# The opening of a recurrence-and-feed-forward kernel, rewritten as an order by hand

## The chip, the cores and the metric

One core of one Trainium2 chip runs the whole kernel. The metric is device time in microseconds, the median of three runs. Kernel inputs are float32 or float64 (the two weights of the first feed-forward layer are float64 and arrive as pairs of 32-bit words). The engines are TensorE (matrix products, PE in the rows), VectorE (DVE), ScalarE (ACT), GpSimd (POOL) and the queue that starts most transfers (SP). Each executes its own instructions in program order.

## The reference

```python
for t in range(S):                      # attention part: 4 batches, 8 heads, 768 steps, 48 wide
    cur = einsum('bhd,bhe->bhde', u[None] * kt, vt)
    y[:, :, t] = einsum('bhd,bhde->bhe', rt, state + cur)
    state = wt[:, :, :, None] * state + einsum('bhd,bhe->bhde', kt, vt)
x = y.transpose(0, 2, 1, 3).reshape(3072, 384)
h = x @ w_in                            # 384 x 2048
x = (h * sigmoid(1.702 * h)) @ w_out    # 2048 x 384
# then: a gate picks one of 8 experts per token, 384 tokens each,
# in order of the logits, and each expert is relu(x @ w1[e]) @ w2[e]
```

## The kernel before, in words

The tokens are cut into 24 **units** of 128 (a chunk of time of one batch) and 8 **blocks** of three units. A unit turns r, k, v, w into 128 rows of x:

- VectorE: two running products of w (the scans, L837 into `Q` and L841 into `Fw`), r*k for the diagonal (L853), k scaled by `Q` (L857), r scaled by `Fw` (L860);
- TensorE: the diagonal (L872), copied by ScalarE to `dg` (L873) and laid on a diagonal by GpSimd (L893); the 128x128 products of k and r (L909); the transposes of k (L928);
- VectorE merges the products into `At` above the diagonal (L916);
- TensorE multiplies `At` with v (L1003, L1009); ScalarE rounds the result to the high part `xh` (L1022) and VectorE subtracts for the low part `xl` (L1024). The state for the next chunk of the batch comes from L945 and L957.

The dense layer then runs block by block, in 16 steps f. A step is a first product `g1` (L1087, nine matmuls: high by high, high by low, low by high), a gelu with a new split into `gh` and `gl` (L1133, L1136, L1139), and a second product `g2` (L1115). Block 0 runs eight steps, then all 16 of block 1, then the rest of block 0.

The weights come in 16 float64 chunks, W0 to W15, alternately of w_in and w_out, 768 KB each. Step f takes the chunk pair f // 2. `split64` turns a chunk into a high and a low float32 part: ScalarE reads the high words (L727), VectorE makes two passes over them (L731, L734) and two over the low words (L740, L741), ScalarE rounds the high part (L745). For W0 to W7 the remainder is formed by TensorE in two halves, three products each (L753 to L755), and moved back by ScalarE (L758); from W8 on VectorE does it (L768, L775).

What stands where in the program is set at build time. `Issue` is a planner: each unit and each chunk is a generator that yields what its last piece costs, and the planner resumes it when its estimate of the engines says so. While it has nothing for TensorE it inserts small products on an identity matrix, `spin` (L691), which keep the engine active and compute nothing that is used. The transfers of the start are in the order of a string:

```python
    ORDER = "0wkr 1wkr W0 2wkr 0v 1v W1 2v 3wkrv 6m"
```

(digits are units, letters their inputs.) The raw chunks land in two buffers `raw64`, so W2 is loaded when W0 is split (L636, through `load_w(m + 2)`). At most eight transfers of the queues are under way: each waits for the landing of the eighth before it.

Of the kernel before, what the change touches and what calls it, by code (L numbers as in the profile page):

```python
# [21 lines left out]
C = 128  # L22
# [478 lines left out]
def kernel(ctx, tc, r, k, v, w, rk, u, us, w_in, w_out, w_gate, w1, w2, out):  # L501
# [44 lines left out]
    LASTF = 3  # L546

# [91 lines left out]

# [17 lines left out]
    ORDER = "0wkr 1wkr W0 2wkr 0v 1v W1 2v 3wkrv 6m"  # L657
    for x in ORDER.split():
        if x[0] == "W":
# [14 lines left out]
    lead = s1p.tile([R2, HP * PW + 1], U8, name="lead")  # L674
    V.memset(lead, 0)
    V.memset(lead[:, ::PW], 1)
    lead2 = s1p.tile([R2, HP * PW], F32, name="lead2")
    V.memset(lead2, 0.0)
# [26 lines left out]

    def split64():
# [3 lines left out]
        def chain(m):  # L710
            while m not in raws:
                yield 0.2
            yield from arrived("raw", m)
            while begun[0] < m:
# [4 lines left out]
            raw = raws.pop(m)  # L719
            low = raw.bitcast(U32).rearrange("p (n two) -> p n two", two=2)[:, :, 0]  # L720
            high = raw.bitcast(I32).rearrange("p (n two) -> p n two", two=2)[:, :, 1]
# [5 lines left out]
            A.activation(a, high.bitcast(F32), AF.Abs, scale=2.0 ** -112)  # L727
            begun[0] = m + 1
            yield (("A", 0.9),)
            yield from sc.room("V", 0.3)  # L730
# [10 lines left out]
            V.scalar_tensor_tensor(Wlo[key] if m < NPE else b, low, 2.0 ** -52, b, op0=OP.mult, op1=OP.mult)  # L741
            if m < NPE:
# [5 lines left out]
                load_w(m + 2)  # L748
# [17 lines left out]
            load_w(m + 2)  # L766
# [13 lines left out]
        for m in range(len(wq)):  # L780
            sc.add(chain(m), SRANK if m < 8 else 2.7)
# [34 lines left out]

    def unit(un):
# [857 lines left out]
```

## Time and profile before

| | |
|---|---|
| median of 3 runs | 852.58 us (852.16 to 854.24) |
| the profiled execution, own time | 854.69 us |
| its span, first to last instruction | 852.7 us |
| TensorE busy | 828.5 us, 97% |
| VectorE busy | 594.6 us, 70% |
| first product of the dense layer (L1087) starts | 39.34 us |
| step f = 2 of block 0 starts | 52.70 us |
| block 1 starts | 107.21 us |

TensorE is nearly always busy by this table, but its busy time holds the `spin` products and whatever runs at half clock. The share of an engine says little on the opening, which is why the times of three landmarks stand beside it: from L1087's first row on, TensorE has the dense layers to do, and before that it waits for x and for weights.

### The profile page before, as it was taken

How to read it: one execution, taken by the hardware profiler on the slowest of the kernel's cores; microseconds unless marked ns; L12 is line 12 of the kernel's file. 1: busy time of each engine (PE TensorE's matmuls, PEld its weight loads, DVE VectorE, ACT ScalarE, POOL GpSimd, SP SyncE). 2: the span in 40 equal slices, each digit the busy share in tenths (PEclk: the TensorE clock that was granted, in tenths of full speed). 3: DMA queues.
4: the chain of work that ended last, by engine and by line, in shares of the span. 5: the costliest groups of instructions: out<-in, count | busy, mean ns of one | idle time of the engine just before them, and what ended most of it. 6: DMA issues, size and time to landing. Idle time of an engine off the chain costs nothing.

```text
span 852.7 us, 17604 instructions
## 1 busy us (share of the span) xinstructions
PE 828.5 (97%) x6789; PEld 776.2 (91%) x6789; DVE 594.6 (70%) x1584; ACT 354.6 (42%) x688; POOL 140.5 (16%) x197
## 2 busy tenths in 40 slices
PE   7999999999999999999999999999999999999996
PEld 6788899999999999999999999997988998999995
DVE  8577578868777775775776856377888887875310
ACT  2254564333233334333333233403566555665521
POOL 3100000010100100100000000002333344445211
PEclk9899999999999999999999999999999999999998
DMA  9623443252321331321322100006989799989400
GB/s 268 178 86 112 162 124 101 64 186 79 112 80 45 104 89 53 96 80 56 103 81 70 46 4 28 1 20 173 225 233 278 214 213 286 264 205 348 98 28 28
DMA packets 46211, 107.04 MB, mean 126 GB/s; under 512 B 7368, under 2 KB 13360, under 8 KB 46128
## 3 DMA queue, kind: packets, MB, share of 16 engines
q1 hardware_dynamic: 30960, 69.26, 25.6%
q0 software_dynamic: 10416, 29.50, 15.8%
q10 hardware_dynamic: 4752, 7.17, 2.3%
q8 instruction: 53, 0.87, 0.4%
q14 instruction: 30, 0.25, 0.1%
HBM read 74.78 MB, written 10.03 MB: 99 GB/s over the span
## 4 chain that ended last, share of the span: by engine, by line
PE 83%; issue 6%; DMA 5%; DVE 3%; ACT 1%; POOL 1%; SPq 0%; POOLq 0%; ACTq 0%; DVEq 0%
PE g L1087 31%; PE acc L1115 31%; PE s L909 3%; PE s L1003 3%; PE s L424 2%; DMA cvb<-x2d,idx 2%; PE s L753 1%; PE s L998 1%; DMA raw<-in_w_out 1%; PE s L1240 1%; PE g L1583 1%; PE acc L691 1%; PE s L945 1%; PE s L1251 1%; PE s L928 1%
## 5 line engine op out<-in xcount | busy, mean ns | idle before, releaser
L1115 PE MATMUL acc<-wk,gh 128*128 128x384 f32 x1080 | 283.3, 341 | 0.1
L1115 PEld LDWEIGHTS acc<-wk,gh 128*128 128x128 f32 x1080 | 192.6, 188 | 3.9 <-issue 3.0
L1115 PE MATMUL acc<-wk,gl 128*128 128x384 f32 x540 | 181.9, 337 | 0.0
L1087 PE MATMUL g<-xha,wk 128*128 128x384 f32 x576 | 167.5, 340 | 0.0
L1087 PE MATMUL g<-xhb,wk 128*128 128x384 f32 x576 | 166.7, 340 | 0.2 <-DVE hold L1139 0.2
L1133 ACT ACTIVATE g<-g 128x384 f32<-128x384 f32 x128 | 60.8, 475 | 212.1 <-PE g L1087 207.7
L1139 DVE TENSOR_TENSOR gl<-g,gh 128x384 fp32r<-128x384 f32 x116 | 64.1, 553 | 64.2 <-ACT gh L1136 63.3
L1087 PEld LDWEIGHTS g<-xhb,wk 128*128 128x128 f32 x576 | 105.8, 189 | 0.8 <-DVE hold L1139 0.5
L1087 PEld LDWEIGHTS g<-xha,wk 128*128 128x128 f32 x576 | 105.6, 188 | 0.5
L1115 PEld LDWEIGHTS acc<-wk,gl 128*128 128x128 f32 x540 | 101.4, 188 | 0.0
L893 POOL TENSOR_SCALAR_AFFINE_SELECT At<-dg 128x512 f32<-128x512 f32 x42 | 31.4, 770 | 414.1 <-DVE dg L886 381.9
L1087 PE MATMUL g<-xlb,wk 128*128 128x384 f32 x288 | 97.4, 338 | 0.0
L1087 PE MATMUL g<-xla,wk 128*128 128x384 f32 x288 | 97.1, 337 | 0.0
L1164 DVE SCALAR_TENSOR_TENSOR cvb<-cva,raw 128x384 f32<-128x384 f32 x144 | 79.3, 551 | 9.6 <-ACT cva L1203 7.3
L1146 ACT ACTIVATE gh<-g 128x384 fp32r<-128x384 f32 x64 | 31.4, 490 | 92.8 <-PE g L1087 86.4
L1149 DVE SCALAR_TENSOR_TENSOR gl<-g,gh 128x384 fp32r<-128x384 f32 x64 | 35.3, 552 | 41.8 <-ACT gh L1146 41.1
L1136 ACT ACTIVATE gh<-g 128x384 fp32r<-128x384 f32 x116 | 57.0, 491 | 7.1 <-ACT cva L1203 2.4
L1466 POOL DMA_DIRECT2D wk<-hold x51 | 46.3, 1014 | 67.4 <-ACT wk L1458 51.9
L1441 ACT ACTIVATE wk<-hold 128x768 fp32r<-128x768 f32 x64 | 52.9, 840 | 7.3 <-DMA hold<-in_w 7.3
L1087 PEld LDWEIGHTS g<-xlb,wk 128*128 128x128 f32 x288 | 54.3, 188 | 0.8 <-issue 0.6
L1087 PEld LDWEIGHTS g<-xla,wk 128*128 128x128 f32 x288 | 54.2, 188 | 0.0
L279 DVE TENSOR_TENSOR cvc<-c,raw 128x768 bf16<-128x768 bf16 x98 | 49.5, 553 | 1.3
(236 smaller groups left out, 1177.1 us busy)
## 6 DMA issues: line engine op xcount, KB each, us to landing
hold<-in_w SPq DMA_DIRECT2D x64, 384.0 KB
wk<-hold POOLq DMA_DIRECT2D x51, 384.0 KB
nat_m<-in_rk SPq DMA_DIRECT2D x18, 384.0 KB
raw<-in_w_in SPq DMA_DIRECT2D x8, 768.0 KB
raw<-in_w_out SPq DMA_DIRECT2D x8, 768.0 KB
nat_v<-in_v SPq DMA_DIRECT2D x22, 256.0 KB
nat_w<-in_w SPq DMA_DIRECT2D x22, 226.2 KB
nat_k<-in_k SPq DMA_DIRECT2D x22, 224.0 KB
```

Source lines behind the costliest of these rows:

```text
L279: self.nc.vector.tensor_tensor(g[:, x:x + step, :n].rearrange("p j (a b) -> p j a b", b=2), self.pairs(c[:, j:j + step], n), self.numbers( ...
L893: P.affine_select(At[s], dg[:, s::2][:, :, None].to_broadcast([128, HP, C]), pattern=[[0, HP], [1, C]], compare_op=OP.is_equal, fill=0.0, ...
L1087: T.matmul(p, self.l1(kt, f, a), (self.xh, self.xl)[b_][:, kt], start=(kt == 0 and n == 0), stop=(kt == KT - 1 and n == 2))
L1115: T.matmul(self.acc[tt], gs[a][:, tt * C:(tt + 1) * C], self.r2(f, b_), start=(f in self.cuts and n == 0), stop=(end and n == 2))
L1133: A.activation(p, p, AF.Gelu_apprx_sigmoid)
L1136: A.activation(gh, p, AF.Copy)
L1139: V.tensor_tensor(gl, p, gh.bitcast(F32), op=OP.subtract)
L1146: A.activation(gh, p, AF.Relu)
L1149: V.scalar_tensor_tensor(gl, p, 0.0, gh.bitcast(F32), op0=OP.max, op1=OP.subtract)
L1164: V.scalar_tensor_tensor(scr[0][:, 0], x2, 1.0, wgB[e // 4][:, (e % 4) * Dm:(e % 4 + 1) * Dm], op0=OP.mult, op1=OP.mult, accum_out=router. ...
L1441: A.activation(Whi[key], raw, AF.Copy)
L1466: P.dma_start(out=Wlo[key].bitcast(F32), in_=raw, accum_op=OP.add)
```

## The change

The first three units leave the planner. A new generator `first_unit` holds what a unit of block 0 does, in pieces, and a string says which piece of which unit (0, 1, 2) or of which chunk (W0, W1) is put next, how many `spin` products go between (s60), and to what the planner's clock is set (@9):

```diff
+    FIRST = ("@9 0 0 s60 0 s4 0 0 1 1 s22 1 0 1 s5 0 2 1 0 0 @16 W0 2 1 2 2 s2 1 1 @20 W0 1 W1 2 2 "
+             "@24 W0 W0 s16 2 2 2 @26 W1 W0 W0 W0 @28")
...
+    APART = 2, 3
...
-        raw = cv.tile([128, KT * CW], I64, name="raw64", bufs=2)
-        nc.sync.dma_start(raw, (w_in if name == "in" else w_out)[i])
-        raws[m] = raw
+        src = (w_in if name == "in" else w_out)[i]
+        if m in APART:
+            n = KT * CW // 2
+            rings = [R["wk"].new() for _ in range(2)]
+            raw = [wpool.tile([128, KT * CW], F32, name="wk") for _ in range(2)]
+            for h in range(2):
+                nc.sync.dma_start(raw[h].bitcast(I32), src[:, h * n:(h + 1) * n].bitcast(I32))
+            raws[m] = raw, rings
+        else:
+            raw = cv.tile([128, KT * CW], I64, name="raw64", bufs=2)
+            nc.sync.dma_start(raw, src)
+            raws[m] = [raw], []
...
+    def next_raw(m):
+        if m not in APART:
+            load_w(m + (4 if m < APART[0] else 2))
...
-    nc.scalar.dma_start(uB, dram(u, 0, [[0, 128], [1, Dm]]))
-    nc.scalar.dma_start(usel, us)
-    ORDER = "0wkr 1wkr W0 2wkr 0v 1v W1 2v 3wkrv 6m"
+    ORDER = "0wkr us 1wkr 0v 2wkr W0 1v 2v W1 W2 W3 3wkrv uB 6m"
...
+    lead = s1p.tile([R2, HP * PW + 1], U8, name="lead")
+    V.memset(lead, 0)
+    V.memset(lead[:, ::PW], 1)
+    lead2 = s1p.tile([R2, HP * PW], F32, name="lead2")
+    V.memset(lead2, 0.0)
     ident = consts.tile([128, 128], F32, name="ident")
...
             begun[0] = m + 1
             yield (("A", 0.9),)
+            while split[0] < min(m, INTURN):
+                yield 0.1
             yield from sc.room("V", 0.3)
             V.tensor_scalar(ai, ai, 3, None, op0=OP.logical_shift_left)
-            yield (("V", 0.56),)
-            yield from sc.room("V", 0.3)
-            V.scalar_tensor_tensor(ai, high, -2147483648, ai, op0=OP.bitwise_and, op1=OP.bitwise_or)
-            yield (("V", 0.99),)
+            for x, c_ in zip(high, cut):
+                V.scalar_tensor_tensor(ai[:, c_], x, -2147483648, ai[:, c_], op0=OP.bitwise_and,
+                                       op1=OP.bitwise_or)
+            yield (("V", 1.55),)
...
-                load_w(m + 2)
+                next_raw(m)
...
     def get_part():
-        while (1, NU - 1) not in stored:
+        while (1, NU - 1) not in stored or split[0] < len(wq):
             yield 0.2
...
     def paced(un):
-        while slot[0] < start[un] or NU - 1 not in half:
+        while slot[0] < start[un] or split[0] < INTURN:
             yield 0.2
...
+    for x in FIRST.split():
+        if x[0] == "s":
+            spin(int(x[1:]))
+        elif x[0] == "@":
+            sc.t = float(x[1:])
+        else:
+            piece(x)
...
-    sc.until(lambda: xdone.get(0) == NU)
...
+        fine[0] = s < begin[2]
```

`first_unit` has the instructions of the old `unit` for a direct unit, with three differences: the products of k and r go into the accumulators of the dense layer (`acc1`, `acc2`) and the output products into a buffer of the first product (`g1`), so that they take none of the three shared buffers `s`; the transposes of k stand right behind the products of k and r; and no `spin` stands inside a group of products. `unit` itself loses its branches for the first three units, and all later units now have the form that only units from 3 on had before (each group of products in one piece). W2 and W3 arrive in two halves each, in buffers of their own, at the start; W4 and W5 then follow W0 and W1. The four passes of VectorE over one chunk of W0 to W3 stand together, since the next chunk waits for its turn. New line numbers: load L618, raw load L652 (halves L648), `spin` L714, first read of a chunk L758, VectorE's passes L764, L766, L773, L775, rounding L783, three products L791 to L793, back L796, scans L874 and L878, r*k L886, diagonal L890, k and r scaled L901 and L902, products L909, transposes L915, merge L922, output products L929 and L933, xh L941, state L946, xl L953, `g1` L1190, `g2` L1218.

On VectorE, from the merge of unit 1 to the first product's last inputs, before:

```order
L916 COPY_PREDICATED wk<-later,s_365 128x512
L916 COPY_PREDICATED wk<-later,s_366 128x512
L853 TENSOR_TENSOR At_401<-wk 112x512
L734 SCALAR_TENSOR_TENSOR cvc<-raw_115,cvc 128x768
L1024 TENSOR_TENSOR xlb<-s_393,xhb 128x3x128
L857 TENSOR_TENSOR wk<-wk,Q 112x512
L860 TENSOR_TENSOR wk<-wk,Fw 112x512
L740 TENSOR_SCALAR cvb<-cvc 128x768
L741 SCALAR_TENSOR_TENSOR wk<-raw_115,cvb 128x768
L916 COPY_PREDICATED At_401<-later,s_462 128x512
L916 COPY_PREDICATED At_402<-later,s_463 128x512
```

and after (cvc, cvb and raw are chunk W0's; At_401 and At_378 are unit 2's):

```order
L922 COPY_PREDICATED wk<-later,acc_316 128x512
L922 COPY_PREDICATED wk<-later,acc_317 128x512
L886 TENSOR_TENSOR At_378<-wk 112x512
L901 TENSOR_TENSOR wk<-wk,Q 112x512
L902 TENSOR_TENSOR wk<-wk,Fw 112x512
L764 TENSOR_SCALAR cvc<-cvc 128x768
L766 SCALAR_TENSOR_TENSOR cvc<-raw_118,cvc 128x768
L953 TENSOR_TENSOR xlb<-g_397,xhb 128x3x128
L922 COPY_PREDICATED At_378<-later,acc_393 128x512
L922 COPY_PREDICATED At_379<-later,acc_394 128x512
L773 TENSOR_SCALAR cvb<-cvc 128x768
L775 SCALAR_TENSOR_TENSOR wk<-raw_118,cvb 128x768
```

Unit 2's scaling of k and r no longer stands behind the wait for unit 1's xh (L1024), and W0's last two passes have moved behind unit 2's merge.

On TensorE, from unit 2's products of k and r (L909) to the dense layer's first product, after (the rows left out are repeats, and 16 `spin` products between L793 and L929):

```order
L909 MATMUL acc_394<-wk 128x128
L915 MATMUL s_439<-ident,wk 128x112 x4
L791 MATMUL s_454<-cvc,ident 128x384
L792 MATMUL s_454<-wk,identr_148 128x384
L793 MATMUL s_454<-wk,identr_147 128x384
...
L929 MATMUL g_474<-At_378,wk 64x128 x2
L933 MATMUL g_474<-At_379,wk 64x128 x2
...
L946 MATMUL s_488<-wk,kn 48x48
L791 MATMUL s_502<-cvc,ident 128x384
L792 MATMUL s_502<-wk,identr_148 128x384
L793 MATMUL s_502<-wk,identr_147 128x384
L1190 MATMUL g_507<-xhb,wk 128x384
```

Before, the two halves of W0's remainder stood between the thirds of unit 2's output products, and its state products (L945) came after the first product had begun. Now one half stands ahead of all output products of unit 2, the other and the state products behind them, all ahead of the first product.

On the queue SP, from the 4th entry on, before (`wk` are unit 2's inputs, `raw` are W0 and W1, the number behind `nat_v` minus 84 is the unit):

```order
L612 DMA nat_w_79<-in_w 112x517
L612 DMA nat_k_83<-in_k 112x512
L612 DMA nat_r_81<-in_r 112x512
L636 DMA raw_115<-in_w_in 128x768
L612 DMA wk<-in_w 112x517
L612 DMA wk<-in_k 112x512
L612 DMA wk<-in_r 112x512
L612 DMA nat_v_84<-in_v 128x512
L612 DMA nat_v_85<-in_v 128x512
L636 DMA raw_122<-in_w_out 128x768
L612 DMA wk<-in_v 128x512
```

and after:

```order
L679 DMA usel<-in_us 112x8
L618 DMA nat_w_79<-in_w 112x517
L618 DMA nat_k_83<-in_k 112x512
L618 DMA nat_r_81<-in_r 112x512
L618 DMA nat_v_84<-in_v 128x512
L618 DMA wk<-in_w 112x517
L618 DMA wk<-in_k 112x512
L618 DMA wk<-in_r 112x512
L652 DMA raw_118<-in_w_in 128x768
L618 DMA nat_v_85<-in_v 128x512
L618 DMA wk<-in_v 128x512
L652 DMA raw_122<-in_w_out 128x768
```

Unit 0's v has passed unit 2's inputs and W0, the small table `usel` has come over from ScalarE's queue, and `uB` (192 KB, used from unit 6 on) has gone from the front of ScalarE's queue to the 22nd place here.

## Rows read from the trace of the kernel before

**Rows 1.** The page, engines: busy us (share of the span) and instructions.

```profile
PE 828.5 (97%) x6789; PEld 776.2 (91%) x6789; DVE 594.6 (70%) x1584; ACT 354.6 (42%) x688; POOL 140.5 (16%) x197
```

**Rows 2.** Timeline of TensorE: start us, us, line, operation, out<-in, count.

```profile
34.69 0.91 PE L753 MATMUL s<-cvc,ident 128*128 128x384 f32 x2
...
35.62 0.34 PE L755 MATMUL s<-wk,identr 128*128 128x384 f32 x1
...
39.34 0.42 PE L1087 MATMUL g<-xhb,wk 128*128 128x384 f32 x1
...
42.24 0.67 PE L945 MATMUL s<-wk,kn 128*64 128x48 f32 x16
...
45.51 2.13 PE L691 MATMUL acc<-ident 128*128 128x128 bf16 x35
...
52.70 0.42 PE L1087 MATMUL g<-xhb,wk 128*128 128x384 f32 x1
...
107.21 0.33 PE L1087 MATMUL g<-xha,wk 128*128 128x384 f32 x1
```

**Rows 3.** VectorE's waits up to the first product: us in total, times, longest.

```profile
DVE xlb L1024 <- ACT xhb L1022: 6.0, 3, 2.4
DVE wk L916 <- PE s L909: 2.4, 1, 2.4
```

**Rows 4.** Timeline of VectorE, units 0 and 1, then chunk W1 and unit 2.

```profile
5.45 1.23 DVE L837 TENSOR_TENSOR_SCAN Q<-nat_w,lead 112x516 f32<-112x516 f32 x1 [0.60 <-DMA nat_w<-in_w]
...
8.08 0.67 DVE L853 TENSOR_TENSOR At<-nat_r,nat_k 112x512 f32<-112x512 f32 x1
...
9.99 1.22 DVE L837 TENSOR_TENSOR_SCAN Q<-nat_w,lead 112x516 f32<-112x516 f32 x1
...
12.66 1.31 DVE L916 COPY_PREDICATED At<-later,s 128x512 f32<-128x512 uint8 x2
...
35.64 0.56 DVE L740 TENSOR_SCALAR cvb<-cvc 128x768 int32<-128x768 int32 x1
36.23 0.96 DVE L741 SCALAR_TENSOR_TENSOR wk<-raw,cvb 128x768 fp32r<-128x768 uint32 x1
39.03 0.56 DVE L1024 TENSOR_TENSOR xlb<-s,xhb 128x384 fp32r<-128x384 f32 x1 [1.84 <-ACT xhb L1022]
```

**Rows 5.** Timeline of TensorE, products of the units, the third at half clock.

```profile
9.35 1.00 PE L872 MATMUL s<-usel,At 112*128 112x2 f32 x8
...
11.50 0.71 PE L909 MATMUL s<-nat_r,nat_k 48*128 48x128 f32 x8
...
22.50 1.23 PE L909 MATMUL s<-nat_r,nat_k 48*128 48x128 f32 x8
...
61.85 1.09 PE L1003 MATMUL s<-wk 128*64 128x128 f32 x16
```

**Rows 6.** Busy us by stretch: PE, PEld, DVE, ACT, POOL, granted clock, DMA, GB/s.

```profile
18.00:20.00 2.00, 2.00 (x24) 1.86 (x23) 0.54 (x2) 0.92 (x3) 0.89 (x2) 1.00 1.05 242
...
21.00:24.00 3.00, 2.98 (x20) 2.22 (x21) 0.59 (x2) 0.00 (x0) 0.47 (x1) 0.51 1.05 280
...
28.00:32.00 4.00, 4.00 (x62) 3.50 (x58) 3.00 (x5) 2.16 (x5) 1.07 (x2) 1.00 0.40 120
...
75.70:79.00 3.30, 3.30 (x11) 2.69 (x10) 3.30 (x7) 1.33 (x3) 0.00 (x0) 0.50 0.50 139
```

**Rows 7.** The `spin` products (L691) alone, by stretch: TensorE busy us (count).

```profile
39.34:52.70 13.36, 3.58 (x49) 2.88 (x49) 1.00 0.31 106
52.70:107.20 54.50, 2.94 (x29) 1.89 (x29) 0.97 0.39 125
```

**Rows 8.** All engines, from step f = 2 to block 1, columns as in rows 6.

```profile
52.70:107.20 54.50, 53.75 (x450) 47.32 (x450) 34.27 (x55) 27.30 (x60) 3.77 (x6) 0.97 0.39 125
```

**Rows 9.** Timeline: W14's last pass on VectorE, and TensorE's first use of it.

```profile
155.23 0.95 DVE L775 TENSOR_TENSOR wk<-cvc,wk 128x768 fp32r<-128x768 f32 x1
...
161.07 0.33 PE L1087 MATMUL g<-xha,wk 128*128 128x384 f32 x1
```

More of the change, by code (lines that the diff above doesn't have):

```diff
@@ L704, in w_done @@
             R["wk"].free(i)
+    by_hand, hands, split = {0, 1}, {}, [0]
     def split64():
@@ L713, in chain @@
             yield from arrived("raw", m)
+            if m not in by_hand:
+                while by_hand:
+                    yield 0.1
             while begun[0] < m:
@@ L896, in unit @@
         sc.busy["P"] += 1.6
-        burst = not direct and un > 2
         last_c = c == NC - 1
         claim[0] += 1
-        while not R["s1"].ok(3 if burst and not last_c else 2):
+        while not R["s1"].ok(2 if last_c else 3):
             yield 0.1
@@ L910, in unit @@
                          start=True, stop=True)
-            if p % PG == PG - 1 and not burst:
-                yield (("T", 0.43 * PG),)
         def select():
@@ L965, in place @@
             return [x[:, :, pos * C:(pos + 1) * C] for x in block_x(blk)]
-        if not burst:
-            select()
-        if not direct:
-            kn = yield from key_rows()
-            half.add(un)
-            yield 0.2
-            free(un, "k")
-        yield from arrived(un, "v")
-        if direct:
-            vs = own["x", un]
-            P.tensor_copy(vs.rearrange("p (s k) d -> p s k d", s=2)[:, :, :, D:],
-                          nv[:, head_at(KT, 0)::2, :D].rearrange("p s (k d) -> p s k d", k=KT))
-            sc.busy["P"] += 0.3
-        two = burst and c
+        kn = yield from key_rows()
+        half.add(un)
+        yield 0.2
+        free(un, "k")
+        yield from arrived(un, "v")
+        two = c > 0
         claim[0] += 1
-        while not R["s1"].ok(1 + two + (burst and not last_c)):
+        while not R["s1"].ok(1 + two + (not last_c)):
             yield 0.1
@@ L999, in unit @@
                                  start=k2 == 0, stop=False, skip_group_check=True)
-        for k in range(KT if direct else HP):
+        for k in range(HP):
             for g in range(2):
@@ L1003, in unit @@
                 T.matmul(out_rows(k, g), nv[:, h], At[h % 2][:, h // 2], start=not c,
[L1004 to L1012 removed]
+                         stop=True, skip_group_check=True)
@@ new lines, in unit @@
+        if kn:
+            pS = yield from state_products(*kn)
+        yield (("T", (1.65 if c else 1.1) + (0.45 if pS else 0.0)),)
+        free(un, "r")
+        yield from wait("y" + sf)
+        iy = R["y" + sf].new()
+        y = buf("y", [128, HP, C]).rearrange("p (k t) -> p k t", k=HP)
+        for n, (ps, done) in enumerate(pys):
+            w_ = HP // len(pys)
+            A.activation(y[:, n * w_:(n + 1) * w_], ps[:, :w_ * C].rearrange("p (k t) -> p k t", k=w_), AF.Copy)
+            done()
@@ new lines, in unit @@
+        sc.busy["A"] += 0.2 * two
+        for s in range(2):
+            for kt in range(KT):
+                (nc.scalar if diag and s else nc.sync).dma_start(
+                    y[64 * s + D:64 * s + 64, kt], y[64 * s + 16 * kt:64 * s + 16 * kt + 16, KT])
+        ty = sc.dma(0.1, (2 - diag) * KT, sc.after((("A", 0.6),)))
+        sc.busy["A"] += 1.1 * diag
+        if pS:
+            state_sum(*pS)
+        free(un, "v")
+        while sc.t < ty:
+            yield 0.1
+        xh, xl = yield from place()
@@ L1326, with piece @@
     split64()
-    for un in range(NUNIT):
-        sc.add(unit(un) if un < NU else paced(un), 1 if un < NU else 2.5 if un < 2 * NU else URANK)
+    for un in range(NU):
+        hands[str(un)] = first_unit(un), 1
+    def piece(name):
+        for _ in range(9):
+            d = next(hands[name][0], None)
+            if isinstance(d, tuple):
+                return
+        assert d is None, (name, sc.t, d)
+    for x in FIRST.split():
[3 more added lines that the diff above has]
+            sc.t = float(x[1:])
+        else:
+            piece(x)
+    assert xdone.get(0) == NU
+    sc.busy.update(V=sc.t, A=sc.t, P=sc.t)
+    for name in [x for x in hands if x[0] == "W"]:
+        sc.add(*hands[name])
+    by_hand.clear()
+    for un in range(NU, NUNIT):
+        sc.add(paced(un), 2.5 if un < 2 * NU else URANK)
     sc.add(gate_weights(), 3)
```

218 lines of the change are left out of this document (139 added, 79 removed).

## The prediction

> **What bounds the kernel now.** I read the page's engines first: TensorE is busy 97% of the span [rows 1], so a gain must come from TensorE time that does nothing useful. That time can't be seen in the share, since `spin` products and half clock count as busy. So I took three landmarks from TensorE's timeline [rows 2]: the dense layer's first product (L1087) at 39.34 us, step f = 2 at 52.70, block 1 at 107.21. From 39.34 on TensorE has the dense layers to do in a fixed order. Whatever moves 39.34 forward moves the end with it, unless something behind it becomes late.
>
> Ahead of 39.34 the limit is a chain over several engines. Of VectorE's waits up to there, three for xh (L1024) make 6.0 us and one for unit 1's products (L916) 2.4 us [rows 3]: 8.4 us in which VectorE, which feeds every unit and every weight chunk, stands behind a value not yet made while other work lies ready behind it. Behind 39.34, `spin` shows what is lost: 49 of them up to f = 2 and 29 more up to block 1 [rows 7]; they step by 0.06 us (35 in 2.1 us [rows 2]), so 2.9 and 1.7 us. Real idle time in that second stretch is only 54.50 - 53.75 = 0.75 us [rows 8]. The granted clock was 0.51 in 21 to 24 us, 1.00 again in 28 to 32, and 0.50 once more in 75.7 to 79 [rows 6]; half is 1.2 of 2.4 GHz.
>
> **The change part by part.** I walk through VectorE's new order with the prices of the rows. *Start:* the first scan began at 5.45 after 0.6 us of waiting for w [rows 4]; it can't begin before 4.85, when VectorE's constants were done. With `uB` gone from the other queue, w has less beside it; I take 5.0, bounds 4.85 and 5.45. *VectorE to unit 2's r*k:* a unit takes 5.45 to 9.99, 4.54 us, of which 2.63 lie ahead of r*k [rows 4]. Two units 9.08, unit 2's scans 2.63, two merges 2 x 1.31, one xl 0.56, one r*k 0.67: 15.6 us, and 0.3 of waiting for unit 0's xh, which now has unit 2's first scan in front of it. So r*k of unit 2 ends at 20.9. Behind it k and r are scaled and W0 gets its first two passes, all of which lie beside TensorE's work.
>
> *TensorE from there:* the diagonal 1.0 [rows 5], unit 1's 24 output products 1.6 (16 take 1.09 [rows 5]), its state 0.67 [rows 2], unit 2's 16 products 1.3 (two rows of 0.71 that overlap [rows 5]): 25.5. Then VectorE's merge 1.31, and W0's last two passes 1.55 (35.64 to 37.19 [rows 4]): 28.4. Here TensorE's order matters: the first half of W0's remainder stands ahead of unit 2's output products and needs the last of these passes, so TensorE waits for it although the merge is done. Its last product 0.2, 16 `spin` 1.0, the output products 1.6, the state 0.67, W0's other half 1.2 (34.69 to 35.96 with the tail of the last [rows 2]): **33.0 us** for the first product at full clock. xh and xl of unit 2 (0.5 and 0.56) lie beside the state and the half chunk; without that cover they would cost 1.1.
>
> *The clock.* In 18 to 20 us TensorE was busy 2.00 of 2.00 us at full clock, much of it with the diagonal, `spin` and small products; at about 21 the granted clock fell, and eight products of k and r went from 0.71 to 1.23 us [rows 5, 6]. The new order has the same kind of work there, fewer `spin` and about 2 us of idle time ahead of unit 2's diagonal, so I expect a fall again. It raises 1.6 + 0.67 + 1.3 by up to 0.73 of itself, 2.6 us, when it lasts as long as the first fall, and half of that when it lasts the 3.3 us of the second one. Between the two I take 34.6 for the first product, nearer the short one, since the idle time comes late in the stretch; bounds are 32.8 (no fall, w at 4.85) and 36.1 (long fall, w at 5.45). **Term 1: 39.34 - 34.6 = 4.7 us.** The Trainium skill (TensorE: Matmul & The Clock Gate, section "What's actually happening") says that half rate is the state at rest and that activity releases it, so fewer `spin` ahead of the first product speak against this change. This trace agrees in that the clock was up through the `spin` of the start; it also fell right behind a stretch that the page shows as fully busy, so the share shown is not the whole of it. By that rule alone the long fall would be taken, and the sum would be 1.0 us poorer.
>
> *Unit 2's state* has passed the first product: 0.6 us less behind it (42.24 to 42.84 [rows 2]). **Term 2: 0.6.** *Steps 0 to 2:* the new program has 37 `spin` where 49 were. W1's, W2's and W3's passes run one behind the other on VectorE, 3.1 us each by my walk, and each ends before TensorE comes to it: W2's last pass at 39 for a product at 39.9, W3's at 42.2 for one at 43, shifted together if the first product is late. W2 and W3 need their raw chunks then; at the 242 GB/s of 18 to 20 us [rows 6] all that is on the queue up to W3, some 6 MB, takes 25 us, so it has landed by 27. So the `spin` cover the waits: 12 x 0.06. **Term 3: 0.7.** W3 is also done here and no longer in the next stretch, which moves work and saves none.
>
> *Up to block 1:* 29 `spin` become 15, 0.85 us. The fall of the clock at 75.7 cost half of 3.4 us, 1.7; whether it comes back is open, since the later units now have their products between dense ones; I count half, 0.85. The idle 0.75 us stay. **Term 4: 1.7.** Bounds -0.5 (a fall, and as much new waiting as one merge takes, 1.31) and 2.6.
>
> *At nothing:* the halves of W2 and W3 (twice as many instructions for the same elements; VectorE has 20 us to spare in 54.5 [rows 8]), the later loads of units 3 on (used some 20 us after they land), `uB`, the late read of the stored part, and the planner's finer steps. Sum 4.7 + 0.6 + 0.7 + 1.7 = **7.7 us**. The profiled execution took 854.69 us by its own time (span 852.7), which would become 847.0; it lies 2.1 us over the median of the runs shown, 852.58, from which I take the same 7.7: **844.9 us**.
>
> **The rivals.** *Given back at the chunks:* W14 was ready at 156.18 and first used at 161.07 [rows 9], 4.9 us of slack. If the late chunks keep their times (transfers and two raw buffers would set them), what exceeds 4.9 us turns into waiting in block 1: 847.7 us. For it: each of W8 to W15 needs VectorE, ScalarE and a buffer in turn. Against: the engines that split were far from full [rows 1, 8], and the order now has W14's last pass behind 17 steps' subtractions where 20 stood before. *The opening doesn't shorten:* the order by hand rests on estimated moments; if VectorE's chain slips (a late landing, a slow GpSimd ahead of a merge), each us moves the first product by one, because W0's half blocks TensorE. From 4.7 us of slip on only terms 2 to 4 could be left, and waits in the place of `spin` eat these: about 851 us. Against: the chain's largest waits are in [rows 3] and none of their causes stands where it stood. *Slower:* the clock falls in the opening and stays at half through the first dense steps, which are bound by TensorE and pay half of every such us. It turns the sign when 15 us more than I count are at half clock, and passes 0.3% from 21 us on; from 21 us to step 2, itself stretched by it, some 26 us more than counted, 13 us of time: about 858. For it: 93 `spin` now stand ahead of unit 2's first products where 137 stood. Against: by 28 us the clock had come back while TensorE was on the same kind of work [rows 6]. The skill's page, named above, would put the return at steady activity, which the dense steps are.
>
> **How the numbers follow.** The forecast 0.68, with a range of its own of 841.5 to 847.5; a gain beyond it, with no fall at all and all of term 4, 0.05; given back 0.15; opening not shorter 0.08; slower 0.04. From 841.0 to 849.0 lie the forecast and most of "given back", 0.8. A change under 0.3% (2.6 us) can hardly be told from none here. Faster by more than that: 0.68 + 0.05 + nearly all of 0.15, 0.86. Within: most of 0.08, 0.09. Slower: 0.05.
>
> **What would show it.** Right: the first L1190 row at 32.5 to 36 us; VectorE without a wait over 1 us from the first scan to W0's second pass; no TensorE wait over 0.5 us between there and block 1, which starts at 98.5 to 101. Wrong: an L792 or L793 row that waits several us for VectorE; the granted clock at 0.50 behind the first product; a wait for a chunk (L783, L796 or L813) in block 1.

## The result, and the profile after

The changed kernel took 844.84 us (median of 4 runs, 842.67 to 845.55) where the kernel before, beside it, took 852.69: a ratio of 0.990, 95% interval 0.988 to 0.992. The forecast was 844.9. The two profiled executions lie further apart than the medians: 842.67 us after, its lowest run, against 854.69 before. Of these 12.0 us the landmarks account for 8.34 up to block 2, after which they run parallel for 340 us; the rest arose between step 127 of the dense layers and the end.

On the page TensorE has 10 us less busy time and the same share as in [rows 1]:

```profile
PE 818.4 (97%) x6719; PEld 770.5 (92%) x6719; DVE 594.3 (71%) x1588; ACT 355.9 (42%) x690; POOL 139.6 (17%) x197
```

TensorE's timeline, the rows that answer to [rows 2] (start, us, line; in brackets the idle time before the row and what ended it):

```profile
20.29 1.84 PE L890 MATMUL s<-usel,At 112*128 112x2 f32 x8 [2.88 <-DVE At L886]
...
27.84 0.82 PE L791 MATMUL s<-cvc,ident 128*128 128x384 f32 x2
29.43 0.44 PE L792 MATMUL s<-wk,identr 128*128 128x384 f32 x1 [0.76 <-ACT wk L783]
30.39 0.44 PE L793 MATMUL s<-wk,identr 128*128 128x384 f32 x1 [0.53 <-DVE wk L775]
30.68 1.07 PE L714 MATMUL acc<-ident 128*128 128x128 bf16 x16
31.67 0.44 PE L929 MATMUL g<-At,wk 128*64 128x128 f32 x4
...
34.68 0.33 PE L1190 MATMUL g<-xhb,wk 128*128 128x384 f32 x1
...
47.36 0.42 PE L1190 MATMUL g<-xhb,wk 128*128 128x384 f32 x1
...
100.18 0.33 PE L1190 MATMUL g<-xha,wk 128*128 128x384 f32 x1
...
199.46 0.33 PE L1190 MATMUL g<-xha,wk 128*128 128x384 f32 x1
```

The first product comes 4.66 us earlier, step f = 2 5.34, block 1 7.03 and block 2 (199.46; before it started at 207.80) 8.34. In the middle of the opening W0's first half stands in TensorE's way, as the prediction had it: transposes done at 28, output products (L929) at 31.67.

VectorE's timeline, which answers to [rows 4]:

```profile
3.86 1.23 DVE L874 TENSOR_TENSOR_SCAN Q<-nat_w,lead 112x516 f32<-112x516 f32 x1 [0.23 <-DMA nat_w<-in_w]
...
14.90 1.65 DVE L874 TENSOR_TENSOR_SCAN Q<-wk,lead 112x516 f32<-112x516 f32 x1
...
19.47 0.68 DVE L886 TENSOR_TENSOR At<-wk 112x512 f32<-112x512 f32 x1
...
25.70 0.56 DVE L953 TENSOR_TENSOR xlb<-g,xhb 128x384 fp32r<-128x384 f32 x1 [2.76 <-ACT xhb L941]
27.57 1.34 DVE L922 COPY_PREDICATED At<-later,acc 128x512 f32<-128x512 uint8 x2 [1.31 <-PE acc L909]
```

It runs from the first scan to W0's second pass (21.98 to 22.94) without a wait. The long waits now lie at 23 to 27.5 us and ahead of unit 2's xl. In the first of them VectorE had work that was ready: W0's last two passes stand behind unit 2's merge, and ScalarE's rounding of W0 stands behind the copy of unit 2's transposes, although both only need the result of W0's second pass. VectorE, then ScalarE:

```profile
21.98 0.96 DVE L766 SCALAR_TENSOR_TENSOR cvc<-raw,cvc 128x768 int32<-128x768 int32 x1
...
28.80 0.54 DVE L773 TENSOR_SCALAR cvb<-cvc 128x768 int32<-128x768 int32 x1
29.38 0.96 DVE L775 SCALAR_TENSOR_TENSOR wk<-raw,cvb 128x768 fp32r<-128x768 uint32 x1
```

```profile
28.10 0.54 ACT L917 ACTIVATE kn<-s 128x448 f32<-128x448 f32 x1 [0.97 <-PE s L915]
28.54 0.83 ACT L783 ACTIVATE wk<-cvc 128x768 fp32r<-128x768 f32 x1
```

TensorE's waits at L792 and L793 are for these two. So W0's half is late through the orders of three engines; e1_half_behind below changes TensorE's alone, and no run moves the other two. The stretches, columns as in [rows 6]; the fourth row is the one that answers to [rows 8]:

```profile
18.00:20.00 2.00, 0.00 (x0) 0.00 (x0) 2.00 (x4) 0.64 (x1) 0.00 (x0) 1.00 1.03 401
21.00:24.00 3.00, 3.00 (x24) 2.80 (x25) 1.90 (x3) 0.18 (x1) 1.50 (x3) 0.50 1.06 237
24.00:26.80 2.80, 2.80 (x36) 2.71 (x34) 0.56 (x1) 1.29 (x3) 0.23 (x2) 0.50 1.07 312
47.36:100.18 52.82, 51.81 (x455) 46.36 (x453) 37.18 (x59) 25.94 (x60) 3.83 (x6) 1.00 0.37 115
```

The clock fell in the opening as before, from 20 to 26.8 us, and not again before the last 5 us of the span. From the first product to f = 2 there are 37 `spin` and from there to block 1 there are 16, against 49 and 29 in [rows 7].

### The profile page after: what moved, and what is told of

Its sections match the earlier page's. It is cut to its first block, busy times and chain, and to the rows that moved or that the text cites. A ratio compares the mean times of both kernels' runs of the same rounds, so it can differ in the third digit from the quotient of the medians.

```text
span 840.6 us, 17468 instructions
## 1 busy us (share of the span) xinstructions
PE 818.4 (97%) x6719; PEld 770.5 (92%) x6719; DVE 594.3 (71%) x1588; ACT 355.9 (42%) x690; POOL 139.6 (17%) x197
## 4 chain that ended last, share of the span: by engine, by line
PE 84%; issue 6%; DVE 4%; DMA 3%; POOL 1%; ACT 1%; POOLq 0%; ACTq 0%; DVEq 0%
PE g L1190 32%; PE acc L1218 31%; PE s L1054 3%; PE s L1136 3%; PE s L424 2%; DMA cvb<-x2d,idx 2%; PE s L1131 1%; PE acc L714 1%; PE s L791 1%; PE s L1354 1%; PE g L1709 1%; PE s L1343 1%; DVE cvb L1267 1%; PE s L1086 1%; PE s L1071 1%
## 5 line engine op out<-in xcount | busy, mean ns | idle before, releaser
L1218 PE MATMUL acc<-wk,gh 128*128 128x384 f32 x1080 | 283.4, 340 | 0.1
L1218 PEld LDWEIGHTS acc<-wk,gh 128*128 128x128 f32 x1080 | 193.4, 188 | 1.5 <-issue 0.8
L1218 PE MATMUL acc<-wk,gl 128*128 128x384 f32 x540 | 182.7, 338 | 0.0
L1190 PE MATMUL g<-xha,wk 128*128 128x384 f32 x576 | 167.1, 340 | 0.0
L1190 PE MATMUL g<-xhb,wk 128*128 128x384 f32 x576 | 165.1, 339 | 0.2 <-DVE hold L1242 0.2
L1190 PEld LDWEIGHTS g<-xha,wk 128*128 128x128 f32 x576 | 105.4, 188 | 0.8 <-issue 0.2
L1190 PEld LDWEIGHTS g<-xhb,wk 128*128 128x128 f32 x576 | 105.2, 188 | 0.7 <-DVE hold L1242 0.5
L1218 PEld LDWEIGHTS acc<-wk,gl 128*128 128x128 f32 x540 | 101.5, 188 | 0.1
L1190 PE MATMUL g<-xla,wk 128*128 128x384 f32 x288 | 97.2, 338 | 0.0
L1190 PE MATMUL g<-xlb,wk 128*128 128x384 f32 x288 | 97.2, 338 | 0.0
L1039 POOL TENSOR_SCALAR_AFFINE_SELECT At<-dg 128x512 f32<-128x512 f32 x38 | 25.8, 700 | 392.3 <-DVE dg L1032 381.8
L1592 POOL DMA_DIRECT2D wk<-hold x51 | 46.4, 1026 | 64.0 <-ACT wk L1584 51.9
L1190 PEld LDWEIGHTS g<-xla,wk 128*128 128x128 f32 x288 | 54.2, 188 | 0.0
L1190 PEld LDWEIGHTS g<-xlb,wk 128*128 128x128 f32 x288 | 54.1, 188 | 0.0
```

Of the source, the lines that this page charges most:

```text
L1039: P.affine_select(At[s], dg[:, s::2][:, :, None].to_broadcast([128, HP, C]), pattern=[[0, HP], [1, C]], compare_op=OP.is_equal, fill=0.0, ...
L1190: T.matmul(p, self.l1(kt, f, a), (self.xh, self.xl)[b_][:, kt], start=(kt == 0 and n == 0), stop=(kt == KT - 1 and n == 2))
L1218: T.matmul(self.acc[tt], gs[a][:, tt * C:(tt + 1) * C], self.r2(f, b_), start=(f in self.cuts and n == 0), stop=(end and n == 2))
L1592: P.dma_start(out=Wlo[key].bitcast(F32), in_=raw, accum_op=OP.add)
```

## The experiments

Every kernel was profiled, and all but b0_again and b1_again (one execution each) were timed beside the kernel before. Three groups ran on three chips, so ratios compare within a group better than across. The landmarks carry most of the weight: behind the first product they repeat to 0.1 us where the clock and the order are alike. A "long" fall of the clock to 0.50 in the opening lasted 6.8 us by the trace, a "short" one 3.4. "Clock up" is read from the first `spin` products: in every trace they start 0.107 us apart at first and 0.056 us apart from this moment on, so up to it TensorE ran at half clock, although the profile's granted clock reads 1.00 on both sides (at a granted clock of 0.50 they are as slow: 16 of them take 1.93 us in e4_v_behind's second fall, 1.07 in after at 1.00).

| kernel | clock up | fall in opening | first product | f = 2 | block 2 | later falls up to there | median us | ratio (95%) |
|---|---|---|---|---|---|---|---|---|
| before | 7.45 | long | 39.34 | 52.70 | 207.80 | at 75.7 | 852.69 | |
| b0_again | 7.78 | long | 39.43 | 52.80 | 207.71 | at 171.6 | 850.26 (1 run) | |
| b1_again | 8.53 | none | 37.45 | 50.80 | 205.84 | at 73.3 | 851.53 (1 run) | |
| e7_before_early | 8.21 | long | 39.91 | 53.27 | 206.58 | | 849.60 | 0.996 (0.994 to 0.999) |
| after | 6.39 | long | 34.68 | 47.36 | 199.46 | | 844.84 | 0.990 (0.988 to 0.992) |
| a0_again | 8.21 | short | 32.85 | 45.54 | 199.20 | at 66.2 | 845.33 | 0.984 (0.981 to 0.988) |
| a1_again | 7.28 | long | 35.26 | 47.95 | 201.66 | at 68.7 | 844.00 | 0.985 (0.982 to 0.988) |
| e1_half_behind | 6.51 | long | 33.30 | 45.86 | 197.99 | | 844.61 | 0.983 (0.979 to 0.986) |
| e2_spins40 | 8.77 | none | 31.72 | 44.37 | 197.22 | | 846.37 | 0.985 (0.982 to 0.989) |
| e3_uB_front | 7.15 | short | 35.76 | 48.43 | 200.55 | | 846.95 | 0.986 (0.983 to 0.990) |
| e4_v_behind | 8.30 | long, short | 37.85 | 50.50 | 202.65 | | 842.83 | 0.988 (0.984 to 0.991) |
| e5_no_early_raw | 6.86 | long | 35.05 | 45.46 | 201.23 | at 61.5 | 841.89 | 0.986 (0.983 to 0.990) |
| e8_both | 8.34 | none | 30.04 | 43.50 | 196.35 | | 843.35 | 0.985 (0.982 to 0.988) |
| e6_no_turns | 9.09 | none | 31.71 | 42.80 | 195.77 | | 842.09 | 0.984 (0.981 to 0.987) |

Group one is a0, e1, e2, e3 (kernel before beside them: 858.39 us); two is b0, e4, e5, e7 (852.71); three is b1, a1, e8, e6 (856.70).

**The changed kernel again (a0_again, a1_again).** No edit.

> The changed kernel once more, as the base for the runs beside it. Mine: 844 to 845 us, and step landmarks that repeat (first product 34.7, block 1 at 100.2, block 2 at 199.5 us); the 3.7 us that the profiled pair gained behind the dense part were chance between two executions, so the expert stage now starts nearer 8.4 than 9.5 us ahead of the kernel before. Rival: they belong to the change, and show again at 12 us.

> The changed kernel as the base for the runs beside it. Mine: first product at 34.7 us with a long fall and 32.9 with a short one, block 2 gains 8.3 to 8.6 on the first trace of before, whole time 843 to 846 us. Rival: these landmarks move by more than the falls of the clock explain.

Measured: the first product follows the fall (short 32.85, long 34.68 and 35.26; of the two long ones the later first product has the fall that starts later, at 20.9 instead of 20.0 us). From there to block 2 it is 164.78 (after), 166.35 and 166.40 us, the last two with one fall each, which is worth 1.6. So block 2 of a1_again gains 6.1 us on the first trace of before and not the 8.3 to 8.6 that I expected: 1.6 is the later fall, 0.6 the opening. The expert stage's start was again 9.5 us ahead in a0_again, not the 8.4 that I expected. From the last dense step to the experts it takes 45.2 to 45.5 us in the three traces of the changed kernel and 46.4, 45.7 and 46.2 in three of the old: 0.2 to 1.2 us that seem to belong to the change. From the start of the experts to the end of the span it is 255.6, 258.5 and 256.6 us, and 258.1, 254.5 and 257.0 in the three traces of the kernel before: no order between the kernels there. The rest of the pair's extra gain is chance between executions.

**The kernel before again (b0_again, b1_again).** No edit.

> The kernel before once more, for its clock: beside the changed kernel it took 855 to 863 us, with a mean granted clock of 0.980 to 0.991, where its first runs took 852 to 854. Mine: its work is the same (step landmarks apart from the stretches at half clock within 0.3 us), and each further stretch of 3.4 us at 0.50 adds 1.7 us; so 858 us shows five or six such stretches where the profiled run of before had three in its opening and dense layers. Rival: the steps themselves are longer, by transfers or waits, at full clock.

> The kernel before once more, to see in which places the granted clock falls in another execution. Mine: one fall of 6.8 us in the opening, as in both traces of before so far, and none to three of 3.4 us at places that differ from execution to execution, each worth 1.5 to 1.7 us; apart from them the step landmarks repeat within 0.3 us. Rival: the later falls sit at fixed steps of the program.

These two executions are the clearest on the clock. Stretches of b0_again (first) and b1_again (second), columns as in [rows 6]:

```profile
20.00:28.00 8.00, 7.27 (x61) 5.00 (x63) 4.34 (x6) 1.36 (x3) 1.61 (x2) 0.59 0.91 236
...
171.60:174.90 3.30, 3.30 (x21) 2.86 (x24) 1.20 (x3) 1.26 (x3) 0.00 (x0) 0.50 0.32 85
```

```profile
20.00:28.00 8.00, 6.75 (x87) 5.08 (x86) 5.34 (x8) 2.58 (x5) 1.68 (x2) 1.00 0.96 239
73.40:76.70 3.30, 3.30 (x11) 2.69 (x12) 3.30 (x6) 1.07 (x2) 0.00 (x0) 0.50 0.48 128
```

The same program went through the opening once at half clock and once at full, and that alone moved its first product from 39.43 to 37.45. An opening without a fall I had not expected. Apart from the falls the landmarks repeat within 0.2 us, as expected. The rival, later falls at fixed steps, is not refuted: whether a later fall comes differs, but in three pairs of traces it comes at nearly the same place. It starts 36.3 us behind the first product in before and 35.9 in b1_again, 33.3 in a0_again and 33.4 in a1_again, and two of them start 125.8 and 159.9 us behind the experts' start in e1_half_behind and 125.4 and 159.5 in e2_spins40. b0_again's at 171.6 and e5_no_early_raw's at 61.5 have no second.

Both executions took only 850 to 852 us, so no trace here shows one of 855 to 863. The recorded clocks bear out my five or six falls there: the mean granted clock was 0.986 in the 11 runs of before in group one, which makes 24 us at half clock; some 5 lie at the end of the span, as in the traces, and 19 us are five to six times 3.4. In group three the mean was 0.988; the changed kernel had 0.9935 and 0.994 beside them. 0.0075 of 856 us is 6.4 us, 0.006 is 5; with them the gain of 8 grows to the 13 that these groups measured. Each run's span times its mean clock is an estimate of the time without falls, if a us at half clock costs half a us: 844.7 and 837.7 us in group one, 844.3 and 837.0 in group three, a gain of 7.0 and 7.3 us.

**Only the early start (e7_before_early).** In the kernel before, the small transfers and constants are moved and nothing else:

```diff
-    nc.scalar.dma_start(uB, dram(u, 0, [[0, 128], [1, Dm]]))
-    nc.scalar.dma_start(usel, us)
-    ORDER = "0wkr 1wkr W0 2wkr 0v 1v W1 2v 3wkrv 6m"
+    ORDER = "0wkr us 1wkr W0 2wkr 0v 1v W1 2v 3wkrv uB 6m"
...
```

The lines left out start `usel` and `uB` on SP at their new places and put the memsets of `lead` and `lead2` ahead of the other constants.

> The kernel before with its small transfers and constants moved as in the change and nothing else. Mine: its first scan starts at 3.7 to 4 instead of 5.45 us, units 0 and 1 run 1.5 us earlier, but three waits for xh and the order of W0 behind unit 2 stay; the first product comes 0.5 to 1.5 us earlier, and with that the total, a fifth or less of the change's 4.7 us. Rival: the early start is most of the change's Term 1; then 3 us or more.

The scan started at 3.68 instead of 5.45, and the first product came at 39.91, 0.6 us later. TensorE's and VectorE's timelines show where the 1.8 us went:

```profile
9.72 1.00 PE L874 MATMUL s<-usel,At 112*128 112x2 f32 x8
...
19.18 0.48 PE L911 MATMUL s<-nat_r,nat_k 48*128 48x128 f32 x2
21.57 1.01 PE L911 MATMUL s<-nat_r,nat_k 48*128 48x128 f32 x6 [1.91 <-ACT kn L934]
```

```profile
12.69 1.34 DVE L918 COPY_PREDICATED At<-later,s 128x512 f32<-128x512 uint8 x2 [1.76 <-PE s L911]
...
24.17 1.34 DVE L918 COPY_PREDICATED wk<-later,s 128x512 f32<-128x512 uint8 x2 [3.31 <-PE s L911]
```

The lead is gone by the merge of unit 0, which starts at 12.69 where it started at 12.66 in [rows 4]: 73 `spin` stand ahead of unit 0's diagonal (L874), so that it starts at 9.72, before at 9.35, and VectorE waits 1.76 us for the products behind it. From there on ScalarE sets the time. In the old order its first read of W1 stands ahead of its copy of unit 1's transposes, which TensorE waits for; before, and in this run:

```profile
19.64 0.90 ACT L727 ACTIVATE cvc<-raw 128x768 f32<-128x768 f32 x1 [0.21 <-DMA raw<-in_w_out]
20.45 0.52 ACT L932 ACTIVATE kn<-s 128x448 f32<-128x448 f32 x1
```

```profile
20.20 0.90 ACT L729 ACTIVATE cvc<-raw 128x768 f32<-128x768 f32 x1 [1.32 <-DMA raw<-in_w_out]
20.99 0.53 ACT L934 ACTIVATE kn<-s 128x448 f32<-128x448 f32 x1
```

W1 landed 0.56 us later here, and the first product came 0.57 us later; from the end of this copy to the first product it takes 18.4 us in all three traces of the old order with a long fall. So VectorE waits 3.3 us for TensorE at unit 1's merge where it waited 2.4 in [rows 3], and the first product loses 0.6 us where I expected a gain of 0.5 to 1.5. The 1.2 us at block 2 are before's fall at 75.7, which is missing here (less the 0.6 lost). The median is 3.1 us below the kernel before beside it, and its interval lies clear of 1, as the rival has it; but the mean clock is 0.9934 against 0.9897, and span times clock is the same, 842.2 against 842.0 us. The early start pays only together with the other edits.

**The start undone (e3_uB_front).** `uB` goes back to the front of ScalarE's queue:

```diff
+    nc.scalar.dma_start(uB, dram(u, 0, [[0, 128], [1, Dm]]))
-    ORDER = "0wkr us 1wkr 0v 2wkr W0 1v 2v W1 W2 W3 3wkrv uB 6m"
+    ORDER = "0wkr us 1wkr 0v 2wkr W0 1v 2v W1 W2 W3 3wkrv 6m"
```

> The transfer of uB goes back to the front of ScalarE's queue. If it was that which made w late before, w lands near 5.3 us and the first scan starts at about 5.4 instead of 3.9: 1.5 us on VectorE's chain, first product 36.2, total +1.5 us. Rival: the new order of constants made the start early and uB takes little: scan at 4 to 4.3, total within 0.3 us. A third outcome: the scan is 1.5 us late and the half clock, which then falls later on the same work, moves with it, so that the first product moves by 0.5 to 2 us.

```profile
6.36 1.23 DVE L875 TENSOR_TENSOR_SCAN Q<-nat_w,lead 112x516 f32<-112x516 f32 x1 [2.72 <-DMA nat_w<-in_w]
```

The scan starts at 6.36, 2.5 to 2.7 us late, more than expected. The first product is at 35.76, 2.9 us behind a0_again, which had a fall of the same length: about one for one. Here, where nothing else blocks the chain, the start counts in full. The short fall moved with the work, from 21.8 to 24.2 us. The median is 1.6 us over a0_again's, about what I expected, though inside the scatter of the runs.

**v behind the weights (e4_v_behind).**

```diff
-    ORDER = "0wkr us 1wkr 0v 2wkr W0 1v 2v W1 W2 W3 3wkrv uB 6m"
+    ORDER = "0wkr us 1wkr W0 2wkr 0v 1v W1 2v W2 W3 3wkrv uB 6m"
```

> Units 0 to 2 get v behind all of w, k, r and W0, as in the kernel before; the order of instructions stays. Mine: v of unit 0 lands at about 15 us where GpSimd wants it from 13.5, and its scaled copy, unit 0's state and the later users move by 1.3 to 1.7 us; first product and total +1.5 us (beside a fall of the clock of the same length). Rival: v is not on the chain that ends last (unit 2's k and r are), so W0 and unit 2's weights, which now come earlier, even help: first product and total within 0.3 us.

GpSimd's waits up to the first product (us in total, times, longest):

```profile
POOL wk L898 <- DMA nat_v<-in_v: 3.2, 1, 3.2
```

In a1_again this wait is 0.4 us. The first product is 3.2 us later than after's. Half of that lies ahead of the second fall, which starts at 32.1 us: the end of W0's first half (L793) starts at 31.97 where it started at 30.39. So the edit costs 1.6, as expected, and the fall the rest; the same difference stands at block 2. The median is no higher than those of the other groups, but on this chip no run of the changed kernel stands beside it.

**No raw buffers of their own (e5_no_early_raw).** W2 and W3 are loaded when W0's and W1's buffers are free:

```diff
-    APART = 2, 3
+    APART = ()
...
-            load_w(m + (4 if m < APART[0] else 2))
+            load_w(m + 2)
...
-    ORDER = "0wkr us 1wkr 0v 2wkr W0 1v 2v W1 W2 W3 3wkrv uB 6m"
+    ORDER = "0wkr us 1wkr 0v 2wkr W0 1v 2v W1 3wkrv uB 6m"
```

> W2 and W3 have no raw buffers of their own: they are loaded when W0's and W1's are free, as in the kernel before, and their splits come later. Mine: VectorE and TensorE wait for them in steps 0 to 2, which take 3 us more (12.7 to 15.7 us from the first product to step f = 2), total +1.5 to +3 us. Rival: the raw chunks come from the free buffers early enough, since W0's is free at 30 us and a chunk lands some 5 us later; then under 0.5 us.

My expectation fell. From the first product to f = 2 it takes 10.41 us instead of 12.68, because W3's products have gone to a later place, and up to block 2 it takes 166.18, which is 164.6 without the fall at 61.5: after's 164.78. Between the first product and f = 2 TensorE waits 0.3 us. The two early raw chunks bring nothing here that the planner doesn't reach without them.

**The two bubbles of the opening (e1_half_behind, e2_spins40, e8_both).** W0's first half goes behind unit 2's output products (e1); 40 `spin` go into the idle time ahead of unit 2's diagonal (e2); both (e8):

```diff
-... 1 0 0 @16 W0 2 1 2 2 s2 1 1 @20 W0 1 W1 2 2 "
-             "@24 W0 W0 s16 2 2 2 @26 W1 W0 W0 W0 @28")
+... 1 0 0 @16 W0 2 1 s40 2 2 s2 1 1 @20 W0 1 W1 2 2 "
+             "@24 W0 s16 2 W0 2 2 @26 W1 W0 W0 W0 @28")
```

> W0's first remainder half goes behind unit 2's output products on TensorE. Mine: it blocks them; they start at about 29 instead of 31.7 us, the state follows, and the first product comes at 33.2 instead of 34.7, so the total falls by about 1.5 us. Rival: unit 2's xl (which waits for ScalarE's xh) is what the first product needs in any case, W0 only fills time; then under 0.3 us. Second rival: W0's halves now come late together, and the total does not fall either.

> 40 spin products in the 2.9 us in which TensorE waits for unit 2's scaled k and r. Theory A, that the idle time behind a busy stretch takes the clock down: it stays at 1.00, diagonal, products and state run at full clock, first product at 32 to 32.5 us, total 2.2 to 2.7 us less. Theory B, that the clock falls after the busy stretch of small products itself (in the kernel before it fell with TensorE busy 2.00 of 2.00 us): the same 6.8 us at 0.50, first product within 0.5 us of 34.7, total unchanged or up to 0.5 us more where spin at half clock are late.

> Both orders together: 40 spin products in the idle time ahead of unit 2's diagonal, and W0's first half behind unit 2's output products. Mine: no fall in the opening, output products of unit 2 at about 26.3 us, first product at 30.2 (31.7 with the spin alone, 33.3 with the half alone), and a dense part 1.5 us shorter than with the spin alone, so that the whole is 2 to 4 us under the changed kernel beside it where later falls of the clock are alike. Rival: what the opening gains comes back as later falls of the clock or as waits for weight chunks in block 1, and the whole is within 1 us of it.

TensorE in e1_half_behind:

```profile
28.93 0.44 PE L929 MATMUL g<-At,wk 128*64 128x128 f32 x4
...
33.30 0.33 PE L1190 MATMUL g<-xhb,wk 128*128 128x384 f32 x1
```

The output products start at 28.93, the first product comes 1.4 to 2.0 us earlier than with the half ahead (at a long fall; 1.4 against after, whose fall starts within 0.2 us of this one), and block 2 1.47 us earlier than in after. The half did block, at the price that I expected, and by the landmarks both rivals fall; the median, 0.7 us under a0_again's, is too coarse to say it. In e2_spins40:

```profile
18.13 2.41 PE L714 MATMUL acc<-ident 128*128 128x128 bf16 x40
20.37 1.00 PE L890 MATMUL s<-usel,At 112*128 112x2 f32 x8
...
31.72 0.34 PE L1190 MATMUL g<-xhb,wk 128*128 128x384 f32 x1
```

No fall; 31.72. That looks like theory A, and the mean clock of the runs is higher than a0_again's (0.9947 against 0.9935), but the median is 1.0 us above a0_again's where A wanted 2.2 to 2.7 less. And e6_no_turns, with the idle time left as it is, has no fall either. Its stretches:

```profile
18.00:20.30 2.30, 0.35 (x13) 0.23 (x7) 2.27 (x5) 1.45 (x3) 0.00 (x0) 1.00 1.05 380
20.30:27.00 6.70, 5.79 (x73) 4.67 (x73) 5.89 (x9) 3.03 (x6) 2.27 (x3) 1.00 1.06 267
```

So idle time does not always take the clock down, and with TensorE kept busy by `spin` it can fall all the same, as before did. With the idle time left, seven of eight traces of the changed opening fell; with `spin` in it none of two. But the column "clock up" separates the fourteen traces without regard to the edits: the clock fell in the opening in all ten in which it came up by 8.30 us, and in none of the four from 8.34 us on, among them b1_again and e6_no_turns, which have no `spin` there. e2_spins40 and e8_both are the other two, so they don't show that their `spin` kept the clock up. A and B stay open, and so does why the two moments go together. In e8_both both edits add up in the opening (30.04, expected 30.2), but the steps behind it become longer. ScalarE's timeline, and TensorE's:

```profile
38.49 0.91 ACT L758 ACTIVATE cvc<-raw 128x768 f32<-128x768 f32 x1 [2.23 <-DMA raw<-in_w_in]
...
39.66 0.86 ACT L783 ACTIVATE wk<-cvc 128x768 fp32r<-128x768 f32 x1
```

```profile
40.56 0.44 PE L792 MATMUL s<-wk,identr 128*128 128x384 f32 x1 [0.64 <-DMA wg<-in_w_gate]
```

ScalarE stands 2.23 us at its first read of W4, whose transfer SP started at 30.84, behind inputs of later units, though W0 had left the buffer at 27.2; after has that row at 40.91 without a wait. W3's rounding (L783) stands behind it in program order, and TensorE's product on it (L792) waits. The releaser that its row names is another transfer, which only ended last by the profile. From the first product to block 2 e8 takes 166.31 us where 164.78 stood: of the 4.64 us ahead of after at the first product 3.11 are left at block 2. Up to block 1 TensorE is idle for 2.2 us where after has 1.0: beside the 0.64 at L792 it waits 0.61 us for a later unit's state (L1054), as it does for 0.65 us in e2_spins40, which takes 165.50 us from its first product to block 2. In the whole time e8 is 0.65 us under a1_again, with overlapping intervals: the rival's "within 1 us". By span times clock it is 0.7 us above a1_again, and e2 1.9 us above a0_again. Where those 3 us went isn't settled. e8 takes 258.8 us from the experts' start to the end of the span, a1 256.6, and in the traces of e1 and e2 two falls stand in that stage; e2's:

```profile
708.60:711.80 3.20, 3.20 (x16) 2.89 (x16) 2.52 (x7) 0.49 (x1) 0.00 (x0) 0.50 1.05 270
742.70:745.90 3.20, 3.20 (x11) 3.20 (x11) 2.47 (x11) 0.00 (x0) 0.11 (x1) 0.50 0.80 167
```

Whether an earlier arrival lengthens the expert stage, the traces are too few to say.

**No turns (e6_no_turns).**

```diff
-    INTURN = 4
+    INTURN = 0
```

> The weight splits no longer take turns from the fourth step on (the planner's old choice); nothing else. Mine: first product and step f = 2 unchanged; block 1 and the total within 0.5 us, since neither order leaves a wait for a chunk in block 1. Rival: without turns a chunk's last pass comes late, TensorE waits in block 1, and the total grows by 1 us or more.

The same number also holds back units 3 and on until four chunks are split, so the edit lifts that too. First product 31.71 without a fall. Step f = 2 is not unchanged: it comes after 11.09 us, since W3's products have gone to a later place. From the first product to block 2 it takes 164.06 us, 0.7 less than after's 164.78 and 1.4 less than the 165.50 of e2_spins40, which has the same first product and no fall either. The total is 1.9 us under a1_again, with intervals that overlap. The rival falls: turn-taking and the hold together gain nothing, and by the landmarks they cost 0.7 to 1.4 us, more than my 0.5.

## Why the prediction was right

The sum of 7.7 us came out, and so did most of its parts; some errors cancel, though. The signs named for it are there in the changed kernel's first trace: first product at 34.68, block 1 at 100.18, no wait of TensorE over 0.35 us between them. One sign of being wrong, the clock at 0.50 behind the first product, came in a0_again and a1_again and cost 1.6 us each.

- *The start* was mis-sized. The scan began at 3.86 and not at 5.0, below my bound of 4.85: in [rows 4] VectorE's constants stood in the way, and I overlooked that the change puts them ahead. VectorE's chain gave part of it back, 16.3 us from the scan to the end of unit 2's r*k where I counted 15.9, since some rows became longer (the scan at 14.90 takes 1.65 us, 1.23 elsewhere). r*k ended at 20.15 instead of 20.9.
- *The full-clock value of the first product* was 33.0 in the sum and is 31.7 (e6_no_turns), 1.3 us less.
- *The clock* cost more than I took: 1.6 us was the middle, a long fall costs 3.0 to 3.6 (34.68 and 35.26 against 31.71), a short one 1.1. It was the long one, and the two errors met at 34.68, where 34.6 stood: that is luck. I also read the clock as up through the `spin` of the start, by the granted clock of 1.00; their spacing shows half clock up to 7.45 us in before. The Trainium skill (TensorE: Matmul & The Clock Gate, section "What's actually happening") has half rate as the state at rest, which activity releases. The `spin` of the start agree with it in every trace, 0.107 us apart at first and 0.056 later. Its use for the opening is not borne out: e6_no_turns, at 1.00 through 2.3 us with 0.35 us of work, and b0_again, at 0.59 in 20 to 28 us while 7.27 of 8.00 us were busy, show that the busy time of the page does not tell whether a fall comes.
- *What bounded the old opening* I named only in part. Beside VectorE's waits of [rows 3] it was the landing of W1, which ScalarE read ahead of unit 1's copy: e7_before_early moved the first product with it, 0.57 us for 0.56. The new order has that read at 26.23 us, behind the copies of units 0 and 1. No run moves it alone, so how Term 1 divides between this read and VectorE's new order is not shown.
- *W0's half* blocked as said: e1_half_behind takes the 1.5 us away.
- *Terms 2 to 4* without the clock were 0.6 + 0.7 + 0.85 = 2.15. From the first product to block 2 it takes 166.67 us in the old order without a fall (e7_before_early) and 164.78 in the new one: 1.9. By stretch it lies elsewhere, 0.7 to f = 2, nothing from there to block 1 and 1.2 in block 1, since work moved between them. The part for the fall at 75.7 was chance: falls at 61 to 76 us stand in two of three traces of before and in three of the ten of the changed kernel and its variants.
- *Like with like*, without any fall: 37.45 + 166.67 = 204.1 for the old order, 31.71 + 164.78 = 196.5 for the new one, 7.6 us. e2_spins40, which has no fall up to there, reached block 2 at 197.22, which makes it 6.9; the estimates by span times clock are 7.0 and 7.3.
- *Costed at nothing*: the raw chunks are worth nothing (e5), the turns with the hold on the later units cost 0.7 to 1.4 (e6). v ahead of the weights is worth 1.6 (e4).
- *Given back at the chunks* did not come: the late chunks did not keep their times. W14's last pass ended at 140.12 us instead of 156.18 and its first use came at 160.38, only 0.7 us earlier, since work was put ahead of it; there is no wait for a chunk in block 1.

Not settled: why before loses more to the clock than the changed kernel in two of the groups, which widens the gain there to 13 us (e7_before_early, the old order with the early start, has the changed kernel's 0.9934 as well); the 0.2 to 1.2 us between dense part and experts.

## What to carry to other kernels

An early start is worth nothing while an engine further down still waits in program order for a transfer that isn't earlier; follow the first result through every engine before pricing it. Price a landmark at full clock and at half apart, and compare traces whose clock fell alike. Before a trace without a fall is put down to an edit, look for traces without the edit that have none either. Once the opening is shorter than the load of the next chunk, what is gained there comes back in part as waiting, at an instruction that stands ahead of the needed one on its engine.

## What the runs showed of the hardware

The granted clock of one and the same program differed from execution to execution. In the opening the old order had no fall or one of 6.8 us at 0.50, the changed kernel one of 3.4 or of 6.8 us, starting between 20.0 and 21.8 us. At the start of every trace the `spin` products were 0.107 us apart up to 6.4 to 9.1 us and 0.056 after that, half clock and full clock, while the profile's granted clock read 1.00; in the ten traces where the change came by 8.30 us the clock fell in the opening, in the four where it came at 8.34 or later it did not; why is not shown. Further falls of 3.4 us, each worth about 1.6 us where TensorE is the limit, came in some executions only; in three pairs of traces they started within 0.5 us of the same place in the program. 2.3 us with TensorE nearly idle passed without a fall in one trace. And `uB`, 192 KB at the front of another queue, delayed the first transfer of w by 2.5 us.
